# Fused Linformer attention and maxout MLP: one activation table set, even tokens first in batch 0, E and F by the plain queue, attention over both PSUM pools

## The chip, the cores and the metric

The kernel runs on one core of one Trainium2 chip. The metric is the device time of one execution in microseconds (us). A run's span is the part of it that the profiler sees, from the first instruction to the last. PE is TensorE (matmuls; PEld its weight loads), ACT is ScalarE, DVE is VectorE, POOL is GpSimd, SP is SyncE. A DMA issued by POOL goes through the software queue, which can convert fp32 to fp16 on the way; one issued by SP goes through the hardware queue and copies bytes as they are (the "plain queue").

## What is computed

Linformer attention over 8 batches and 8 heads, and behind it a maxout MLP on the 8192 tokens.

```python
# q, k, v: (8, 8, 1024, 64) fp32; E, F: (64, 1024); w1, w2: (512, 1024); w_out: (1024, 512)
k_proj = np.einsum('ks,bhsd->bhkd', E, k)
v_proj = np.einsum('ks,bhsd->bhkd', F, v)
scores = (1.0 / np.sqrt(64)) * np.matmul(q, k_proj.transpose(0, 1, 3, 2))
scores = scores - np.max(scores, axis=-1, keepdims=True)
attn = np.exp(scores)
attn = attn / (np.sum(attn, axis=-1, keepdims=True) + 1e-09)
attn_out = np.matmul(attn, v_proj)
x = attn_out.transpose(0, 2, 1, 3).reshape(8192, 512)
out = np.maximum(x @ w1, x @ w2) @ w_out        # (8192, 512) fp32
```

## The kernel before

All matmuls are fp16 with fp32 sums in PSUM. The order on every engine is the order in which the program is written (`manual_schedule`); semaphores follow from the tiles that instructions share.

**Attention of one batch** has these steps. `step_kv` (line 127): 16 matmuls give `k_proj` in partitions 0 to 63 and `v_proj` in 64 to 127 of one PSUM tile; ACT casts the first to `kp`, DVE the second, twice, to both halves of `vp`. `step_kpt` (line 145) transposes `kp` on PE; ACT and DVE copy it to `kpt`. Then for each of four pairs of heads p: `step_qt` (line 162) transposes the pair's q by eight PE transposes and DVE copies it to `qt`; `step_sc` (line 179) makes the scores with four matmuls and ACT takes their exponential to `ex`; `step_da` (line 195) makes the denominators (matmuls with a matrix of ones, into `dn_ps`) and the unnormalised result (into `at_ps`). The reciprocal is exp(-ln(x)): ACT computes `ld` (line 212, Ln) and `rec` (line 213, Exp). The multiply on DVE into `xt` (line 216) is returned as `finish` and is put into the program later. Token s is at partition s//8 and chunk s%8; the last axis but one of `xt` is the token's parity: even chunks at 0, odd chunks at 1.

**The MLP of one batch** is 24 blocks (`moe_blocks`, line 223), twelve for the even tokens (j=0), then twelve for the odd ones (j=1). An up block is eight matmuls, four for `w2` and four for `w1`, into two PSUM banks; ACT copies the first bank to `h2` (line 241), DVE takes the maximum with the second (line 242) into `gt`. After eight up blocks come four down blocks of eight matmuls (line 250), an ACT copy to `o_sb` (line 257) and an output DMA by SP. So blocks 0 to 7 and 12 to 19 are up, 8 to 11 and 20 to 23 down.

**PSUM** has eight banks in two rings. Tag "mm": four tiles of one bank, taken by MLP blocks alone. Tag "att": two tiles of two banks, taken in turn by every attention step, the transposes included. A new tile waits until the readers of the tile that had its place are done.

**The order.** Ahead of the loop the whole attention of batch 0 runs by itself, in two groups of four heads, pair after pair, each finished before the next begins (the head of the program). Then batch b's MLP blocks run, and between them stand the attention steps of batch b+1, by the table `plan` (block number to steps); a `finish` comes after the next block. The kernel's last batch has no attention beside it. POOL issues E and F first (lines 66, 67), then k, v, q of batch 0 in halves of four heads (line 76), the weights (line 92, in eight pieces; line 96), then builds the identity matrix for the transposes, and then loads the next batches as their buffers come free.

Of the kernel before, what the change touches and what calls it, by code (L numbers as in the profile page):

```python
# [8 lines left out]
FP32 = mybir.dt.float32  # L9
FP16 = mybir.dt.float16  # L10
ACTF = mybir.ActivationFunctionType
ALU = mybir.AluOpType
# [3 lines left out]
def kernel(  # L16
# [24 lines left out]

    scale = 1.0 / float(D) ** 0.5
# [3 lines left out]
    proj = ctx.enter_context(tc.tile_pool(name="proj", bufs=2))  # L46
    soft = ctx.enter_context(tc.tile_pool(name="soft", bufs=2))
    xpool = ctx.enter_context(tc.tile_pool(name="xpool", bufs=2))
    gpool = ctx.enter_context(tc.tile_pool(name="gpool", bufs=2))
# [40 lines left out]
    for f0 in range(0, DF, 256):  # L90
        for w_sb, w in ((w1_sb, moe_w1), (w2_sb, moe_w2)):
# [6 lines left out]
    ident16 = const.tile([128, 128], FP16)  # L98
    make_identity(nc, ident16)
    ones16 = const.tile([128, D], FP16)  # L100
    nc.vector.memset(ones16, 1.0)


    eft = const.tile([128, 2, NC, KP], FP16)
    ef_v = ef_sb.rearrange("kp i (p c) -> kp i c p", c=NC)
    eft_ps = att_banks(FP16)
    for i in range(2):
        for c in range(NC):
            nc.tensor.transpose(  # L109
                out=eft_ps[:, i, c * KP : (c + 1) * KP],  # L110
                in_=ef_v[:, i, c, :],
                identity=ident16[:KP, :KP],
            )
        nc.vector.tensor_copy(
            out=eft[:, i, :, :].rearrange("p c k -> p (c k)"), in_=eft_ps[:, i, 0 : NC * KP]
        )

# [8 lines left out]

    def step_kv(t, h0=0, h1=None):
        h1 = H if h1 is None else h1
        n = (h1 - h0) * D
        kv_ps = att_banks()  # L130
        for c in range(NC):
            nc.tensor.matmul(  # L132
                out=kv_ps[0:KP, 0, 0:n], lhsT=eft[:, 0, c, :], rhs=t["k"][:, h0:h1, c, :],
                start=(c == 0), stop=(c == NC - 1),
            )
            nc.tensor.matmul(  # L136
                out=kv_ps[KP:128, 0, 0:n], lhsT=eft[:, 1, c, :], rhs=t["v"][:, h0:h1, c, :],
                start=(c == 0), stop=(c == NC - 1),
            )
        fl = lambda ap: ap.rearrange("p h d -> p (h d)")  # L140
        nc.scalar.copy(out=fl(t["kp"][:, h0:h1, :]), in_=kv_ps[0:KP, 0, 0:n])  # L141
        nc.vector.tensor_copy(out=fl(t["vp"][KP:128, h0:h1, :]), in_=kv_ps[KP:128, 0, 0:n])
        nc.vector.tensor_copy(out=fl(t["vp"][0:KP, h0:h1, :]), in_=kv_ps[KP:128, 0, 0:n])

    def step_kpt(t, p0=0, p1=None):
        p1 = NP2 if p1 is None else p1
        kpt_ps = att_banks(FP16)
        for p in range(p0, p1):
            nc.tensor.transpose(
                out=kpt_ps[:, 0, p * KP : (p + 1) * KP],  # L150
                in_=t["kp"][:, 2 * p : 2 * p + 2, :],
                identity=ident16[:KP, :KP],
            )
        src = kpt_ps[:, 0, 0 : NP2 * KP].rearrange("q (p k) -> q p k", k=KP)
        dst = t["kpt"].rearrange("q (p e) k -> q p e k", e=2)
        for e in range(2):
            for r in range(2):
                eng = nc.scalar.copy if e == 0 else nc.vector.tensor_copy
                eng(
                    out=dst[r * D : (r + 1) * D, p0:p1, e, :],  # L160
                    in_=src[e * D : (e + 1) * D, p0:p1, :],
                )

    def step_qt(t, p):
        qt_ps = att_banks(FP16)
        for e in range(2):
            for i in range(NI):
                nc.tensor.transpose(  # L168
                    out=qt_ps[:, 0, (e * NI + i) * 128 : (e * NI + i + 1) * 128],
                    in_=t["q"][:, 2 * p + e, 2 * i : 2 * i + 2, :],  # L170
                    identity=ident16,
                )
        qt = soft.tile([128, 2, HALF], FP16, tag="qt", name="qt_sb")
        t["qt"][p] = qt
        nc.vector.tensor_copy(out=qt.rearrange("q e n -> q (e n)"), in_=qt_ps[:, 0, :])  # L175

    def step_sc(t, p):
        sc_ps = att_banks()  # L180
        qt = t["qt"].pop(p)
        for o in range(2):
            for e in range(2):
# [6 lines left out]
                )  # L190
        ex = soft.tile([128, 2, HALF], FP16, tag="ex", name="ex_sb")
        t["ex"][p] = ex
        nc.scalar.activation(out=ex, in_=sc_ps, func=ACTF.Exp, scale=scale)  # L193

    def step_da(t, p):
# [19 lines left out]
        def finish():  # L215
            nc.vector.tensor_tensor(  # L216
                out=t["xt"][:, p, :, :], in0=at_ps, in1=rec, op=ALU.mult
            )

# [66 lines left out]

    for b in range(B):
# [7 lines left out]
        for n, block in enumerate(moe_blocks(b, tiles[b])):  # L295
            block()
            if pending is not None:
                pending()
                pending = None
            if nxt is None:  # L300
                continue
            for s in plan.get(n, ()):
                if isinstance(s, tuple):
                    r = s[0](nxt, s[1])
                else:
                    r = s(nxt)
                if r is not None:
                    pending = r
# [31 lines left out]
```

## Time and profile before

| | |
|---|---|
| time, median of 3 runs | 506.37 us (505.75 to 507.42) |
| time of the profiled execution | 505.09 us |
| its span | 503.1 us |
| instructions | 5945 |
| HBM read, written | 57.15 MB, 16.78 MB |
| software queue (POOL's loads) | 30432 packets, 28.58 MB, 36.8% of 16 engines' span |
| hardware queue (SP's stores) | 9216 packets, 16.78 MB, 8.7% |
| PE matmuls of the up blocks (L234) | 1024, 382 ns each |
| PE matmuls of the down blocks (L250) | 512, 379 ns each |
| ACT table loads (L212 and L213) | 32 and 32, 1283 ns each |

Matmuls are pipelined: one begins while the one before still drains, so a row's duration is longer than the step from one to the next. The "idle before" of a row is the time that its engine stood with nothing running ahead of it, and the name behind the arrow is what ended that. A timeline row gives the start, the time, the engine, line and operation, the tiles (written<-read), shapes and count.

### The profile page before, as it was taken

The page shows a single profiled execution, that of the slowest core. Times are in us where ns is not written, and L with a number is a line of the kernel's source. Part 1 is how long each engine was busy: PE and PEld are TensorE (multiplying, and loading weights), DVE is VectorE, ACT ScalarE, POOL GpSimd, SP SyncE. Part 2 cuts the span into 40 slices and gives each one's busy share as a digit, 9 for nine tenths or more (in the row PEclk, how much of TensorE's full clock was granted, in tenths as well). Part 3 has the DMA queues.
Part 4 walks back from the last instruction along what each step waited for, and adds up shares of the span by engine and source line. Part 5 has one row for each costly group of instructions (what it writes and reads, how often), then busy time and mean ns, then how long its engine had stood idle before and what let it go on. Part 6 is the DMA issues. An engine that isn't in the chain of part 4 may idle for free.

```text
span 503.1 us, 5945 instructions
## 1 busy us (share of the span) xinstructions
PE 416.8 (83%) x2368; PEld 181.7 (36%) x2368; DVE 162.5 (32%) x231; ACT 296.7 (59%) x380; POOL 31.5 (6%) x44
## 2 busy tenths in 40 slices
PE   0053379888997999888988999889988999799997
PEld 0032124333443344333433344333433344334443
DVE  0023225242514334233524243242524252342231
ACT  1036644788367753887366854876467845866332
POOL 6321000000100010000100010000000000000000
PEclk9999999999999999999999999999999999999999
DMA  8999949233761629152751549152020011102112
GB/s 127 201 201 207 207 79 165 87 45 77 130 126 43 97 77 169 76 78 90 111 120 24 103 96 177 44 83 85 0 85 1 22 63 43 42 1 83 43 42 83
DMA packets 39675, 45.73 MB, mean 91 GB/s; under 512 B 1632, under 2 KB 31328, under 8 KB 39648
## 3 DMA queue, kind: packets, MB, share of 16 engines
q0 software_dynamic: 30432, 28.58, 36.8%
q1 hardware_dynamic: 9216, 16.78, 8.7%
q8 instruction: 18, 0.29, 0.2%
q14 instruction: 9, 0.07, 0.0%
HBM read 57.15 MB, written 16.78 MB: 147 GB/s over the span
## 4 chain that ended last, share of the span: by engine, by line
PE 48%; ACT 28%; issue 11%; DVE 8%; DMA 3%; POOL 1%; ACTq 0%; POOLq 0%
PE mm_ps L234 32%; PE mm_ps L250 8%; ACT L212 8%; ACT ld_sb L212 7%; DVE xt_sb L216 6%; ACT rec_sb L213 5%; DMA w_sb<-in_moe_w_dram 3%; PE att_ps L168 3%; ACT h_sb L241 3%; PE att_ps L132 3%; ACT ex_sb L193 2%; ACT o_sb L257 2%; ACT L213 1%; PE att_ps L185 1%; DVE gt_sb L242 1%
## 5 line engine op out<-in xcount | busy, mean ns | idle before, releaser
L234 PE MATMUL mm_ps<-xt_sb,w_sb 128*128 128x512 f16 x1024 | 238.1, 382 | 4.6 <-DVE xt_sb L216 4.0
L234 PEld LDWEIGHTS <-w_sb 128*128 128x128 f16 x1024 | 95.7, 98 | 126.4 <-issue 24.2
L242 DVE TENSOR_TENSOR gt_sb<-mm_ps,h_sb 128x512 f16<-128x512 f32 x128 | 88.4, 691 | 159.8 <-PE mm_ps L234 100.0
L241 ACT COPY h_sb<-mm_ps 128x512 f32<-128x512 f32 x128 | 74.8, 584 | 91.0 <-PE mm_ps L234 91.0
L250 PE MATMUL mm_ps<-wo_sb,gt_sb 128*128 128x512 f16 x512 | 118.0, 379 | 8.5 <-DVE gt_sb L242 5.5
L216 DVE TENSOR_TENSOR xt_sb<-att_ps,rec_sb 128x1024 f16<-128x1024 f32 x32 | 39.1, 1221 | 121.9 <-ACT rec_sb L213 121.9
L250 PEld LDWEIGHTS <-gt_sb 128*128 128x128 f16 x512 | 48.0, 98 | 73.5 <-issue 12.3
L257 ACT COPY o_sb<-mm_ps 128x512 f32<-128x512 f32 x64 | 35.9, 584 | 46.7 <-PE mm_ps L250 46.7
L193 ACT ACTIVATE ex_sb<-att_ps 128x1024 f16<-128x1024 f32 x32 | 32.9, 1027 | 14.9 <-PE att_ps L185 14.9
L213 ACT ACT_TABLE_LOAD x32 | 41.1, 1283 | 0.6
L212 ACT ACT_TABLE_LOAD x32 | 41.1, 1283 | 0.6
L168 PE MATMUL att_ps<-ident,q_sb 128*128 128x128 f16 x256 | 21.1, 229 | 22.9 <-DVE xt_sb L216 9.7
L213 ACT ACTIVATE rec_sb<-ld_sb 128x1024 f32<-128x1024 f32 x32 | 33.8, 1057 | 0.4
L212 ACT ACTIVATE ld_sb<-att_ps 128x1024 f32<-128x1024 f32 x32 | 32.8, 1024 | 0.4
L168 PEld LDWEIGHTS <-q_sb 128*128 128x128 f16 x256 | 18.2, 102 | 33.5 <-issue 28.4
L141 ACT CAST kp_sb<-att_ps 64x512 f16<-64x512 f32 (+1 forms) x9 | 4.8, 530 | 42.9 <-PE att_ps L136 42.9
L185 PE MATMUL att_ps<-qt_sb,kpt_sb 64*64 64x512 f16 x128 | 14.0, 426 | 12.5 <-DVE qt_sb L175 8.2
L175 DVE COPY qt_sb<-att_ps 128x1024 f16<-128x1024 f16 x32 | 21.9, 684 | 6.1 <-PE att_ps L168 6.1
L109 PE MATMUL att_ps<-ident,ef_sb 64*128 64x64 f16 x16 | 1.3, 241 | 26.1 <-POOL ident masks.py:199 25.6
L132 PE MATMUL att_ps<-k_sb,eft 128*64 128x512 f16 (+1 forms) x72 | 17.4, 390 | 1.3 <-ACT ld_sb L212 1.3
L76 POOL DMA_DIRECT2D q_sb<-in_q_dram x9 | 7.7, 855 | 163.3 <-PE att_ps L168 162.8
L204 PE MATMUL att_ps<-ex_sb,ones 64*64 64x512 f16 x128 | 14.0, 427 | 4.5 <-ACT ex_sb L193 4.5
(29 smaller groups left out, 114.4 us busy)
## 6 DMA issues: line engine op xcount, KB each, us to landing
out_dram<-o_sb SPq DMA_DIRECT2D x64, 256.0 KB, 2.0
k_sb<-in_k_dram POOLq DMA_DIRECT2D x7, 1024.0 KB, 9.3
v_sb<-in_v_dram POOLq DMA_DIRECT2D x7, 1024.0 KB, 14.0
q_sb<-in_q_dram POOLq DMA_DIRECT2D x7, 1024.0 KB, 9.4
w_sb<-in_moe_w_dram POOLq DMA_DIRECT2D x8, 256.0 KB, 14.6
k_sb<-in_k_dram POOLq DMA_DIRECT2D x2, 512.0 KB, 10.0
v_sb<-in_v_dram POOLq DMA_DIRECT2D x2, 512.0 KB, 11.8
q_sb<-in_q_dram POOLq DMA_DIRECT2D x2, 512.0 KB, 13.6
```

What stands on the lines that cost most here:

```text
L132: nc.tensor.matmul(out=kv_ps[0:KP, 0, 0:n], lhsT=eft[:, 0, c, :], rhs=t["k"][:, h0:h1, c, :], start=(c == 0), stop=(c == NC - 1),)
L168: nc.tensor.transpose(out=qt_ps[:, 0, (e * NI + i) * 128 : (e * NI + i + 1) * 128], in_=t["q"][:, 2 * p + e, 2 * i : 2 * i + 2, :], identi ...
L175: nc.vector.tensor_copy(out=qt.rearrange("q e n -> q (e n)"), in_=qt_ps[:, 0, :])
L193: nc.scalar.activation(out=ex, in_=sc_ps, func=ACTF.Exp, scale=scale)
L212: nc.scalar.activation(out=ld, in_=dn_ps, func=ACTF.Ln)
L213: nc.scalar.activation(out=rec, in_=ld, func=ACTF.Exp, scale=-1.0)
L216: nc.vector.tensor_tensor(out=t["xt"][:, p, :, :], in0=at_ps, in1=rec, op=ALU.mult)
L234: nc.tensor.matmul(out=h_ps, lhsT=w_sb[:, r, fb * 128 : (fb + 1) * 128], rhs=xt[:, r, j, :], start=(r == 0), stop=(r == NDC - 1),)
L241: nc.scalar.copy(out=h2, in_=banks[0])
L242: nc.vector.tensor_tensor(out=gt[:, fb, :], in0=banks[1], in1=h2, op=ALU.max)
L250: nc.tensor.matmul(out=op_ps, lhsT=gt[:, fb, i * 128 : (i + 1) * 128], rhs=wo_sb[:, fb, :], start=(fb == 0), stop=(fb == NFB - 1),)
L257: nc.scalar.copy(out=o_sb, in_=op_ps)
```

## The change

**Tables.** ACT loads one table set (number 6, with Ln and Exp) by hand as its first instruction. **E and F** come as fp32 by SP's queue, are transposed as fp32, and cast to fp16 as they leave PSUM, E's by DVE and F's by ACT. **The identity** is built after the first two loads that POOL issues; DVE makes its fp16 copy. **Batch 0's loads** are k and v in halves, then q in four pieces of two heads; for each slice of weights `w2` comes ahead of `w1`. **PSUM.** `step_kv`, `step_kpt`, `step_qt` and the transposes of E and F take a bank of the "mm" ring; scores and denominators keep the "att" ring. **Batch 0's attention** runs for all eight heads at once; the steps for pair p+1 stand ahead of the second half of pair p; and ahead of the MLP only the even tokens are finished, by `step_da_half` (denominators and result in one tile, half as wide). The odd tokens of pair n follow behind MLP block n. `ex` has four buffers for that. **The plan**: `step_kv` moves from block 1 to 4, `step_kpt` from 3 to 6, and most later steps by one to four blocks.

```diff
-    def mm_bank():
-        return ps.tile([128, 512], FP32, tag="mm", bufs=4, name="mm_ps")
-
-    def att_banks(dtype=FP32):
+    def mm_bank(dtype=FP32):
         return ps.tile(
-            [128, 2, 512 if dtype == FP32 else 1024], dtype, tag="att", bufs=2, name="att_ps"
+            [128, 512 if dtype == FP32 else 1024], dtype, tag="mm", bufs=4, name="mm_ps"
         )
 
+    def att_banks():
+        return ps.tile([128, 2, 512], FP32, tag="att", bufs=2, name="att_ps")
...
+    nc.scalar.add_instruction(
+        mybir.InstLoadActFuncSet(
+            name=nc.get_next_instruction_name(),
+            act_func_set_id=LN_EXP_SET,
...
-    ef_sb = const.tile([KP, 2, S], FP16)
-    nc.gpsimd.dma_start(out=ef_sb[:, 0, :], in_=E)
-    nc.gpsimd.dma_start(out=ef_sb[:, 1, :], in_=F)
+    ef_sb = const.tile([KP, 2, S], FP32)
+    nc.sync.dma_start(out=ef_sb[:, 0, :], in_=E)
+    nc.sync.dma_start(out=ef_sb[:, 1, :], in_=F)
...
-        load(tiles[0], "q", q, 0, h0, h0 + H // 2)
+        if h0 == 0:
+            ident = const.tile([128, 128], FP32)
+            make_identity(nc, ident)
+    for h0 in range(0, H, 2):
+        load(tiles[0], "q", q, 0, h0, h0 + 2)
...
+    def step_da_half(t, p, o):
+        ex = t["ex"][p]
+        da_ps = att_banks()
+        for i in range(2):
+            for e in range(2):
+                r = o ^ e
+                rows = slice(r * KP, (r + 1) * KP)
+                nc.tensor.matmul(
+                    out=da_ps[e * D : (e + 1) * D, i, :],
+                    lhsT=t["vp"][rows, 2 * p + e, :] if i else ones16[rows, :],
+                    rhs=ex[rows, e, :],
+                    start=True, stop=True,
+                )
+        ld = soft.tile([128, HALF], FP32, tag="ldh", name="ldh_sb")
+        rec = soft.tile([128, HALF], FP32, tag="rech", name="rech_sb")
+        nc.scalar.activation(out=ld, in_=da_ps[:, 0, :], func=ACTF.Ln)
+        nc.scalar.activation(out=rec, in_=ld, func=ACTF.Exp, scale=-1.0)
+
+        def finish():
+            nc.vector.tensor_tensor(
+                out=t["xt"][:, p, o, :], in0=da_ps[:, 1, :], in1=rec, op=ALU.mult
+            )
...
-    hh = H // 2
-    fins = []
-    for g in range(2):
-        step_kv(t, g * hh, (g + 1) * hh)
-        step_kpt(t, g * hh // 2, (g + 1) * hh // 2)
-        for p in range(g * hh // 2, (g + 1) * hh // 2):
-            step_qt(t, p)
-            step_sc(t, p)
-            step_da(t, p)()
-
+    step_kv(t)
+    step_kpt(t)
+    step_qt(t, 0)
+    step_sc(t, 0)
+    for p in range(NP2):
+        if p + 1 < NP2:
+            step_qt(t, p + 1)
+            step_sc(t, p + 1)
+        step_da_half(t, p, 0)()
+
+    first = {n: (step_da_half, n, 1) for n in range(NP2)}
     plan = {
-        1: [step_kv], 3: [step_kpt],
-        4: [(step_qt, 0)], 6: [(step_sc, 0)], 7: [(step_qt, 1)], 9: [(step_da, 0)],
-        10: [(step_sc, 1)], 11: [(step_qt, 2)], 13: [(step_da, 1)],
-        14: [(step_sc, 2)], 15: [(step_qt, 3)], 17: [(step_da, 2)],
+        4: [(step_kv,)], 6: [(step_kpt,)], 7: [(step_qt, 0)], 8: [(step_sc, 0)],
+        9: [(step_qt, 1)], 11: [(step_da, 0)], 12: [(step_sc, 1)], 13: [(step_qt, 2)],
+        14: [(step_da, 1)], 15: [(step_sc, 2)], 16: [(step_qt, 3)], 17: [(step_da, 2)],
         18: [(step_sc, 3)], 20: [(step_da, 3)],
     }
```

**What moves, on POOL.** These are POOL's first rows of the program before, from the second transfer on (the first is E's, L66); `ident_108` is the fp16 identity, whose two instructions are those of masks.py.

```order
L67 DMA ef_sb<-in_F_dram 64x1024
L76 DMA k_sb<-in_k_dram 128x4x512
L76 DMA v_sb<-in_v_dram 128x4x512
L76 DMA q_sb<-in_q_dram 128x4x512
L76 DMA k_sb<-in_k_dram 128x4x512
L76 DMA v_sb<-in_v_dram 128x4x512
L76 DMA q_sb<-in_q_dram 128x4x512
L92 DMA w_sb<-in_moe_w_dram 128x4x256 x8
L96 DMA wo_sb<-in_moe_w_out_dram 128x8x512
masks.py:197 MEMSET ident_108 128x128
masks.py:199 ISA
masks.py:199 AFFINE_SELECT ident_108<-ident_108 128x128
```

The same place in the changed program:

```order
L89 DMA k_sb<-in_k_dram 128x4x512
L89 DMA v_sb<-in_v_dram 128x4x512
masks.py:197 MEMSET ident 128x128
masks.py:199 ISA
masks.py:199 AFFINE_SELECT ident<-ident 128x128
L89 DMA k_sb<-in_k_dram 128x4x512
L89 DMA v_sb<-in_v_dram 128x4x512
L89 DMA q_sb<-in_q_dram 128x2x512 x4
L109 DMA w_sb<-in_moe_w_dram 128x4x256 x8
L113 DMA wo_sb<-in_moe_w_out_dram 128x8x512
```

The identity moved from behind seventeen transfers to behind two, the second half of v from seventh place in POOL's queue to fourth, and E and F left the queue.

**On ACT, in the head.** Before, one pair of heads after another (two of the four pairs are shown):

```order
L193 ACTIVATE ex_sb<-att_ps 128x1024
L212 ACT_TABLE_LOAD
L212 ACTIVATE ld_sb<-att_ps 128x1024
L213 ACT_TABLE_LOAD
L213 ACTIVATE rec_sb<-ld_sb 128x1024
L193 ACTIVATE ex_sb<-att_ps 128x1024
L212 ACT_TABLE_LOAD
```

And now, from the first exponentials on (`ldh` and `rech` are the half-width tiles of `step_da_half`):

```order
L205 ACTIVATE ex_sb<-att_ps 128x1024 x2
L250 ACTIVATE ldh_sb<-att_ps 128x512
L251 ACTIVATE rech_sb<-ldh_sb 128x512
L205 ACTIVATE ex_sb<-att_ps 128x1024
L250 ACTIVATE ldh_sb<-att_ps 128x512
L251 ACTIVATE rech_sb<-ldh_sb 128x512
L205 ACTIVATE ex_sb<-att_ps 128x1024
```

The table loads are gone, the logarithm and the reciprocal are half as wide, and the exponential of pair p+1 stands ahead of those of pair p.

**On ACT, in the loop**, from the last down blocks of the even tokens into the up blocks of the odd ones. Before:

```order
L257 COPY o_sb<-mm_ps 128x512 x2
L212 ACT_TABLE_LOAD
L212 ACTIVATE ld_sb<-att_ps 128x1024
L213 ACT_TABLE_LOAD
L213 ACTIVATE rec_sb<-ld_sb 128x1024
L257 COPY o_sb<-mm_ps 128x512
L193 ACTIVATE ex_sb<-att_ps 128x1024
L257 COPY o_sb<-mm_ps 128x512
L241 COPY h_sb<-mm_ps 128x512 x2
```

And now:

```order
L295 COPY o_sb<-mm_ps 128x512 x3
L224 ACTIVATE ld_sb<-att_ps 128x1024
L225 ACTIVATE rec_sb<-ld_sb 128x1024
L279 COPY h_sb<-mm_ps 128x512
L205 ACTIVATE ex_sb<-att_ps 128x1024
L279 COPY h_sb<-mm_ps 128x512 x2
L224 ACTIVATE ld_sb<-att_ps 128x1024
```

The first `step_da` moved from behind block 9 to behind block 11, its two table loads are gone, and one MLP block still stands between it and the next scores.

More of the change, by code (lines that the diff above doesn't have):

```diff
@@ L10 @@
 FP16 = mybir.dt.float16
+LN_EXP_SET = 6
 ACTF = mybir.ActivationFunctionType
@@ L90 @@
     for f0 in range(0, DF, 256):
-        for w_sb, w in ((w1_sb, moe_w1), (w2_sb, moe_w2)):
+        for w_sb, w in ((w2_sb, moe_w2), (w1_sb, moe_w1)):
             nc.gpsimd.dma_start(
@@ L96 @@
     nc.gpsimd.dma_start(out=wo_sb, in_=moe_w_out.rearrange("(r p) f -> p r f", p=128))
[L98 to L99 removed]
     ones16 = const.tile([128, D], FP16)
     nc.vector.memset(ones16, 1.0)
+    ident16 = const.tile([128, 128], FP16)
+    nc.vector.tensor_copy(out=ident16, in_=ident)
     eft = const.tile([128, 2, NC, KP], FP16)
     ef_v = ef_sb.rearrange("kp i (p c) -> kp i c p", c=NC)
[L106 removed]
     for i in range(2):
+        eft_ps = mm_bank()
         for c in range(NC):
             nc.tensor.transpose(
[L110 removed]
+                out=eft_ps[:, c * KP : (c + 1) * KP],
                 in_=ef_v[:, i, c, :],
[L112 removed]
+                identity=ident[:KP, :KP],
             )
[L114 to L116 removed]
+        eng = nc.scalar.copy if i else nc.vector.tensor_copy
+        eng(out=eft[:, i, :, :].rearrange("p c k -> p (c k)"), in_=eft_ps)
     def new_attn(t):
@@ L125, in new_attn, with step_kv, step_kpt @@
         t["ex"] = {}
[L127 to L130, printed above, removed]
+    def step_kv(t):
+        kv_ps = mm_bank()
         for c in range(NC):
[L132 to L139, printed above, removed]
-        fl = lambda ap: ap.rearrange("p h d -> p (h d)")
[L141 to L148, printed above, removed]
+            for i, n in enumerate(("k", "v")):
+                nc.tensor.matmul(
+                    out=kv_ps[i * KP : (i + 1) * KP, :],
+                    lhsT=eft[:, i, c, :],
+                    rhs=t[n][:, :, c, :],
+                    start=(c == 0), stop=(c == NC - 1),
+                )
+        fl = lambda ap: ap.rearrange("p h d -> p (h d)")
+        nc.scalar.copy(out=fl(t["kp"]), in_=kv_ps[0:KP, :])
+        nc.vector.tensor_copy(out=fl(t["vp"][KP:128]), in_=kv_ps[KP:128, :])
+        nc.vector.tensor_copy(out=fl(t["vp"][0:KP]), in_=kv_ps[KP:128, :])
+    def step_kpt(t):
+        kpt_ps = mm_bank(FP16)
+        for p in range(NP2):
             nc.tensor.transpose(
-                out=kpt_ps[:, 0, p * KP : (p + 1) * KP],
+                out=kpt_ps[:, p * KP : (p + 1) * KP],
                 in_=t["kp"][:, 2 * p : 2 * p + 2, :],
@@ L190, in step_sc @@
                 )
-        ex = soft.tile([128, 2, HALF], FP16, tag="ex", name="ex_sb")
+        ex = stage.tile([128, 2, HALF], FP16, tag="ex", name="ex_sb")
         t["ex"][p] = ex
@@ L299 @@
                 pending = None
+            if b == 0 and n in first:
+                s = first[n]
+                pending = s[0](tiles[0], *s[1:])
             if nxt is None:
```

26 lines of the change are left out of this document (16 added, 10 removed).

## The prediction

> **What bounds the kernel now.** First the busy times with the span cut at the places where the MLP of a batch gets its last input (the start of the matmuls that wait for the fourth pair's `xt`): the head in two rows, the first batch, one of six equal ones, and the last with the tail.
>
> ```profile
> 0.00:25.60 25.60, 0.01 (x1) 0.14 (x2) 0.11 (x1) 1.28 (x1) 13.25 (x24) 1.00 1.07 165
> 25.60:68.00 42.40, 18.33 (x136) 9.85 (x136) 10.94 (x18) 24.34 (x26) 5.16 (x6) 1.00 1.26 203
> 67.97:125.26 57.29, 52.56 (x292) 22.27 (x292) 20.05 (x28) 36.58 (x47) 2.63 (x3) 1.00 0.43 79
> 180.81:236.37 55.56, 50.83 (x293) 21.87 (x293) 20.05 (x28) 36.73 (x48) 2.62 (x3) 1.00 0.48 95
> 458.57:503.10 44.53, 40.95 (x189) 18.38 (x188) 11.07 (x16) 14.22 (x25) 0.00 (x0) 0.98 0.17 65
> ```
>
> Columns are the stretch and its length, busy time of PE, PEld, DVE, ACT and POOL, the granted clock, DMA share and GB/s. There are two programs in one: a head of 68 us in which PE works 18 us, and a loop in which PE works 50.8 of 55.6 us and everything else has room (ACT 36.7, DVE 20.1). In the loop only PE's idle time can go; in the head nearly all can. So next, what PE waits for (us in total, times, longest):
>
> ```profile
> PE att_ps L109 <- POOL ident masks.py:199: 25.6, 1, 25.6
> PE att_ps L168 <- DVE xt_sb L216: 9.7, 7, 1.4
> PE att_ps L168 <- ACT ex_sb L193: 9.5, 7, 1.4
> PE mm_ps L250 <- DVE gt_sb L242: 5.5, 7, 0.8
> PE att_ps L185 <- ACT ld_sb L212: 4.3, 7, 0.6
> PE mm_ps L234 <- DVE xt_sb L216: 4.0, 4, 3.5
> PE mm_ps L250 <- ACT h_sb L241: 3.0, 7, 0.4
> ```
>
> 25.6 us go to the identity, which POOL builds behind all of the first loads. Five waits come seven times each, once per batch with attention beside it: 9.7 + 9.5 + 5.5 + 4.3 + 3.0 = 32.0 us. The timeline shows their cause, with a stretch without a wait for comparison:
>
> ```profile
> 195.07 0.41 PE L185 MATMUL att_ps<-qt_sb,kpt_sb 64*64 64x512 f16 x4
> 195.41 1.90 PE L234 MATMUL mm_ps<-xt_sb,w_sb 128*128 128x512 f16 x8
> 197.15 0.61 PE L168 MATMUL att_ps<-ident,q_sb 128*128 128x128 f16 x8
> ...
> 201.15 0.41 PE L204 MATMUL att_ps<-ex_sb,ones 64*64 64x512 f16 x4
> 201.70 1.90 PE L250 MATMUL mm_ps<-wo_sb,gt_sb 128*128 128x512 f16 x8
> 201.86 1.28 ACT L212 ACT_TABLE_LOAD   x1
> 203.15 1.02 ACT L212 ACTIVATE ld_sb<-att_ps 128x1024 f32<-128x1024 f32 x1
> 204.22 0.41 PE L185 MATMUL att_ps<-qt_sb,kpt_sb 64*64 64x512 f16 x4 [0.62 <-ACT ld_sb L212]
> 205.49 1.06 ACT L213 ACTIVATE rec_sb<-ld_sb 128x1024 f32<-128x1024 f32 x1
> 206.57 1.22 DVE L216 TENSOR_TENSOR xt_sb<-att_ps,rec_sb 128x1024 f16<-128x1024 f32 x1 [7.86 <-ACT rec_sb L213]
> 207.85 0.61 PE L168 MATMUL att_ps<-ident,q_sb 128*128 128x128 f16 x8 [1.38 <-DVE xt_sb L216]
> ```
>
> Unhindered, eight matmuls take 1.74 us from start to start (195.41 to 197.15) although the row says 1.90; the 0.16 between is drain that overlaps. So each wait costs 0.16 more than its row says. With table loads between, ACT needs 4.7 us from 201.86 to hand `rec` to DVE, and PE stands at every "att" tile that has to come free.
>
> **The change: the loop.** The five waits are 32.0/7 = 4.57 us a batch, plus 5 x 0.16 = 5.37. The matmuls that open a batch wait too: (4.0 - 3.5)/3 = 0.17, plus 0.16. Together 5.7 us a batch; 55.56 - 5.7 leaves 49.86. PE's own instructions per batch stay the same, only their places change.
>
> Are the waits gone, and what is late next? I walk the queues with the durations above. (1) Scores behind `ld`: the denominators take 0.41 from 201.15; an ACT copy of 0.58 goes ahead, ready 0.2 later by the drain, so `ld` runs 0.8 to 1.8 after the first of these matmuls. PE wants that tile one block later, at 0.55 + 1.74 = 2.29. Early by 0.5. (2) The q transposes leave the "att" ring. They now wait for the bank that is four allocations back: for the third pair, behind block 13, that is the `h2` bank of block 12, free when ACT has done `ld`, `rec` (1.06) and the copy (0.58), at 3.5; wanted two blocks and the scores later, at 4.37. Early by 0.9. (3) Down block 20, the next late one: its eighth matmul needs `gt` of block 19. From the third pair's denominators: `rec` until 2.5, copy of block 18 until 3.1, maximum (0.69) until 3.85, the multiply (1.22) until 5.1, maximum of block 19 until 5.8. PE comes to it after two blocks and the scores, 4.37, and seven matmuls, 1.52: 5.89. Early by under 0.1. It costs nothing by this walk, but a delay on DVE there is paid in full, seven times. MLP blocks share their ring with six more tiles a batch; the tightest reuse is the first bank of a block that takes the `w1` bank of two blocks before, 1.74 us after it is filled; the maximum is normally done 0.16 + 0.69 later, so DVE may be 0.9 late. The multiplies take 1.22 but stand behind that maximum in DVE's queue, so I cost the sharing at nothing. Seven batches: **-39.9 us**.
>
> **The change: the head.** Rows for its links (issue and landing of the two transfers that fix them, the durations at full width, and one pair of before):
>
> ```profile
> 4.65 0.79 POOL L76 DMA_DIRECT2D k_sb<-in_k_dram  x1
> k_sb<-in_k_dram POOLq DMA_DIRECT2D x1, 512.0 KB, 12.7
> L109 PE MATMUL att_ps<-ident,ef_sb 64*128 64x64 f16 x16 | 1.3, 241 | 26.1 <-POOL ident masks.py:199 25.6 <-DVE eft L114 0.5
> 26.72 0.88 POOL L76 DMA_DIRECT2D v_sb<-in_v_dram  x1 [0.33 <-DMA w_sb<-in_moe_w_dram]
> v_sb<-in_v_dram POOLq DMA_DIRECT2D x1, 1024.0 KB, 21.6
> 67.97 4.70 PE L234 MATMUL mm_ps<-xt_sb,w_sb 128*128 128x512 f16 x13 [3.50 <-DVE xt_sb L216]
> L141 ACT CAST kp_sb<-att_ps 64x512 f16<-64x512 f32 x7 | 4.1, 579 | 15.0 <-PE att_ps L136 15.0
> L142 DVE CAST vp_sb<-att_ps 64x512 f16<-64x512 f32 x7 | 4.9, 694 | 12.0 <-ACT kp_sb L141 12.0
> L159 DVE COPY kpt_sb<-att_ps 64x256 f16<-64x256 f16 x14 | 4.1, 293 | 1.5 <-ACT kpt_sb L159 1.4
> L175 DVE COPY qt_sb<-att_ps 128x1024 f16<-128x1024 f16 x32 | 21.9, 684 | 6.1 <-PE att_ps L168 6.1
> L241 ACT COPY h_sb<-mm_ps 128x512 f32<-128x512 f32 x128 | 74.8, 584 | 91.0 <-PE mm_ps L234 91.0
> L242 DVE TENSOR_TENSOR gt_sb<-mm_ps,h_sb 128x512 f16<-128x512 f32 x128 | 88.4, 691 | 159.8 <-PE mm_ps L234 100.0
> 31.20 1.01 PE L168 MATMUL att_ps<-ident,q_sb 128*128 128x128 f16 x8 [0.61 <-DVE vp_sb L143]
> 41.41 0.64 PE L185 MATMUL att_ps<-qt_sb,kpt_sb 64*64 64x512 f16 x4 [3.21 <-DVE qt_sb L175]
> 42.10 1.02 ACT L193 ACTIVATE ex_sb<-att_ps 128x1024 f16<-128x1024 f32 x1 [2.60 <-PE att_ps L185]
> 47.86 1.23 DVE L216 TENSOR_TENSOR xt_sb<-att_ps,rec_sb 128x1024 f16<-128x1024 f32 x1 [6.50 <-ACT rec_sb L213]
> ```
>
> *Loads.* The identity is ready within 4 us; what ends last is then the second half of v. It stands fourth among k, v and q as k's second half did, which landed at 4.65 + 12.7 = 17.35. POOL reaches its first load sooner by two issues, at most 2 x 0.79 us; E and F as fp32 put twice their 0.26 MB into SBUF, some 1.3 us more at the 203 GB/s of the second window. I set the one against the other and take 17.4; the ends are 15.8 (the extra bytes are hidden) and 19.9 (none of the issue time comes back and E and F go ahead at full length). The Trainium skill, "Trainium Kernel Development and Optimization", section Key Constraints, says that DMAs issued from different engines run on the same 16 DMA engines and interleave, and that another queue only saves issue time. By it the bytes of E and F still count, which is the value taken; were SP's queue a second road, 15.8 would stand. Transposes of fp32 have no row; the 16 fp16 ones of L109 are 1.3 us of PE, and even five times that lies in PE's idle time between the identity and 17.4. That wait is their cover.
>
> *Chain.* In the head PE runs at half its pace: 13 matmuls take 4.70 us at 67.97, where the loop's 1.74 for eight makes 2.8, and four score matmuls take 0.64 instead of 0.41. So `step_kv`, eight pairs at twice 0.22, ends with its drain 3.8 after the landing, at 21.2. Then `kp` 0.58, two `vp` casts, 2 x 0.69, two `kpt` copies, 2 x 0.29, `qt` 0.68, scores 0.64: with 0.05 per hand-over the first exponential starts 4.1 later. The second follows 2.5 behind it (1.01 of transposes beside 1.02 of Exp, copy, scores). From there a pair takes Exp 1.02, `ld` and `rec` at half width, 2 x 0.58 (no row shows them; they lie between zero and the 1.02 of full width, and the nearest row is the copy of that width, 584 ns), multiply 0.69 (the nearest row, L242), `qt` 0.68, scores 0.64 and hand-overs: 4.35; before, the way from Exp to the end of the multiply alone took 42.10 to 49.09, 7.0. Two such, then Exp, four half-width ACT passes and a multiply, 4.1. Sum 4.1 + 2.5 + 8.7 + 4.1 = 19.4, so the MLP has its last even input at 40.6 instead of 67.97: **-27.4 us**. All eight half-width passes are on this chain: at 1.02 they add 3.5, at nothing they take 4.6 off. With the ends of the landing it lies between 34 and 47.
>
> *Beside the MLP.* The odd halves add four groups of four matmuls, each like the scores, 0.34 (195.07 to 195.41): **+1.4 us**. The next batch's v lands at 26.72 + 21.6 = 48.3; batch 0 asks for it five blocks in, at about 52. Weights land before that, so no transfer becomes late, with some 4 us in hand.
>
> **The sum** is made against the profiled execution: 503.1 - 39.9 - 27.4 + 1.4 = 437.2 us of span; around the span lie 505.09 - 503.1 = 2.0 us, so 439.2; the median of the runs is 1.3 above the profiled one: **440 us**.
>
> **The rivals.** *PE warms in the head.* The half pace shows in the durations of the head (the granted-clock column says 1.00 all the same), and the gaps ahead of its rows are 3.21 and 3.50 us. The new head has no gap over about 2 us. If PE ran at the loop's pace there, the scores would gain 0.23 in four pairs, and the first batch its extra 57.29 - 55.56 = 1.7: 2.7 us off, 437. For it: the shorter gaps. Against: PE stays barely half busy. The Trainium skill, "TensorE: Matmul & The Clock Gate", Part 1, puts the rule so: PE runs at half rate until some 3.4 us of sustained work, and falls back after as long a gap. By that the shorter gaps help only once it is warm.
>
> *A new wait in the loop.* ACT and DVE come late to the "mm" banks or to down block 20, because transposes and MLP now draw on one ring. For it: margins of 0.1 to 0.9. Against: with ACT at 36.7 - 8 x 1.28 = 26.5 of 50 us, delays don't pile up. If between a fifth and half of the 5.7 comes back, 7 x 1.1 to 7 x 2.9 = 8 to 20 us: 448 to 460.
>
> *The waits stay.* The loads go but PE's order, not ACT, made the waits: only the head gains, 480. Against it: the `ld` wait is half the length of one table load. The order of ACT shows a single load in the changed program, so that part does what it says.
>
> *Slower: the clock.* A loop without gaps could make the chip throttle PE. The gain of 66 us is lost when a loop of some 394 us (53.0 for the first batch, 6 x 49.86, 42 for the last) takes 17% longer; at the half pace of the head it would add over 300. Against it: the last batch ran 42 us with PE at work nearly throughout, at a granted 0.98. The same page of the Trainium skill says that a limit to 13/16 comes only with a third busy core on a die; no run here shows it.
>
> **Chances.** Forecast 0.62 (434 to 447, by the ends of the head); warm PE 0.12; new wait 0.20; waits stay 0.04; slower 0.02. The range takes the first two and the nearer half of the third: 434 to 455. A measurement tells 0.3% from no change; faster by more than that is 0.98, within it 0, slower 0.02.
>
> **What would show it.** In the changed profile: one ACT_TABLE_LOAD; the first `step_kv` matmul near 17.4; the MLP's 13-matmul row near 40.6; ex-to-ex steps of 4.35 in the head; a batch period of 49.9; no wait of PE that comes seven times, or else first the one of the down blocks on `gt`. I am wrong if the period stays above 51, if v lands past 20, or if a row of `ldh` is much longer than 0.6.

## The result and the profile after

| | before | changed |
|---|---|---|
| time, median | 506.06 us (504.67 to 507.42, 4 runs) | 439.42 us (439.28 to 439.81, 4 runs) |
| profiled execution, its span | 505.09, 503.1 us | 439.34, 437.6 us |
| ratio, 95% interval | | 0.8685 (0.866 to 0.8709) |

The change takes 66.6 us off. The same two views as before, of the changed kernel: stretches of the span (the first MLP, then one period of the loop, from the matmuls right behind one batch's `step_kv` to the same place of the next), and what PE waits for (the five longest of eight rows).

```profile
38.80:92.37 53.57, 53.57 (x305) 21.91 (x305) 22.25 (x32) 30.30 (x46) 2.64 (x3) 1.00 1.09 196
102.95:152.89 49.94, 49.94 (x295) 21.77 (x293) 19.86 (x28) 26.43 (x39) 2.63 (x3) 1.00 0.53 106
```

```profile
PE mm_ps L147 <- DMA k_sb<-in_k_dram: 6.6, 1, 6.6
PE att_ps L197 <- DVE qt_sb L187: 5.7, 4, 1.8
PE mm_ps L126 <- DMA ef_sb<-in_E_dram: 4.6, 1, 4.6
PE mm_ps L147 <- DMA v_sb<-in_v_dram: 1.9, 1, 1.9
PE mm_ps L272 <- DVE xt_sb L254: 0.7, 1, 0.7
```

The second column of the stretches (the length) and the first busy time (PE) are now the same number: by this profile PE never stands still in the loop. All five waits that came seven times are gone; every wait that is left lies in the head. There, the timeline of PE and ACT (a choice of its rows) shows the chain that the prediction walked:

```profile
16.10 0.60 PE L147 MATMUL mm_ps<-v_sb,eft 128*64 128x512 f16 x1 [1.89 <-DMA v_sb<-in_v_dram]
19.73 0.58 ACT L154 CAST kp_sb<-mm_ps 64x512 f16<-64x512 f32 x1 [12.10 <-PE mm_ps L147]
23.72 1.02 ACT L205 ACTIVATE ex_sb<-att_ps 128x1024 f16<-128x1024 f32 x1 [2.17 <-PE att_ps L197]
26.11 1.02 ACT L205 ACTIVATE ex_sb<-att_ps 128x1024 f16<-128x1024 f32 x1 [1.37 <-PE att_ps L197]
30.35 1.02 ACT L205 ACTIVATE ex_sb<-att_ps 128x1024 f16<-128x1024 f32 x1 [2.07 <-PE att_ps L197]
34.59 1.02 ACT L205 ACTIVATE ex_sb<-att_ps 128x1024 f16<-128x1024 f32 x1 [2.07 <-PE att_ps L197]
36.77 0.60 ACT L250 ACTIVATE ldh_sb<-att_ps 128x512 f32<-128x512 f32 x1
38.80 2.29 PE L272 MATMUL mm_ps<-xt_sb,w_sb 128*128 128x512 f16 x5 [0.67 <-DVE xt_sb L254]
41.03 0.63 PE L242 MATMUL att_ps<-ex_sb,ones 64*64 64x512 f16 x2
42.02 2.06 PE L272 MATMUL mm_ps<-xt_sb,w_sb 128*128 128x512 f16 x8
44.01 0.40 PE L242 MATMUL att_ps<-ex_sb,ones 64*64 64x512 f16 x2
44.25 0.38 PE L242 MATMUL att_ps<-ex_sb,vp_sb 64*64 64x512 f16 x2
44.56 1.90 PE L272 MATMUL mm_ps<-xt_sb,w_sb 128*128 128x512 f16 x8
```

The MLP has its last input at 38.80 instead of 67.97.

### The profile page after: what moved, and what is told of

The parts are those of the page before. It is cut to its first block, busy times and chain, and to the rows that moved or that the text cites. A ratio compares the mean times of both kernels' runs of the same rounds, so it can differ in the third digit from the quotient of the medians.

```text
span 437.6 us, 5860 instructions
## 1 busy us (share of the span) xinstructions
PE 413.1 (94%) x2352; PEld 180.3 (41%) x2352; DVE 160.7 (37%) x231; ACT 215.4 (49%) x322; POOL 31.8 (7%) x44
## 4 chain that ended last, share of the span: by engine, by line
PE 92%; DMA 3%; ACT 2%; DVE 1%; issue 1%; POOL 1%; POOLq 0%
PE mm_ps L272 52%; PE mm_ps L288 26%; PE mm_ps L147 4%; PE att_ps L216 4%; PE mm_ps L180 3%; PE att_ps L197 3%; DMA v_sb<-in_v_dram 3%; ACT ex_sb L205 1%; DVE qt_sb L187 1%; PE att_ps L242 1%; ACT rech_sb L251 1%; ACT ldh_sb L250 1%; PE mm_ps L161 0%; POOL k_sb L89 0%; DVE xt_sb L254 0%
## 5 line engine op out<-in xcount | busy, mean ns | idle before, releaser
L228 DVE TENSOR_TENSOR xt_sb<-att_ps,rec_sb 128x1024 f16<-128x1024 f32 x28 | 34.1, 1217 | 24.7 <-ACT rec_sb L225 24.7
L187 DVE COPY qt_sb<-mm_ps 128x1024 f16<-128x1024 f16 x32 | 21.9, 683 | 25.8 <-PE mm_ps L180 25.7
L225 ACT ACTIVATE rec_sb<-ld_sb 128x1024 f32<-128x1024 f32 x28 | 29.6, 1057 | 0.9
L147 PE MATMUL mm_ps<-k_sb,eft 128*64 128x512 f16 x64 | 17.2, 413 | 6.6 <-DMA k_sb<-in_k_dram 6.6
L180 PE MATMUL mm_ps<-ident,q_sb 128*128 128x128 f16 x256 | 21.2, 230 | 0.0
L147 PE MATMUL mm_ps<-v_sb,eft 128*64 128x512 f16 x64 | 17.0, 413 | 1.9 <-DMA v_sb<-in_v_dram 1.9
L154 ACT CAST kp_sb<-mm_ps 64x512 f16<-64x512 f32 x8 | 4.6, 579 | 26.9 <-PE mm_ps L147 26.9
L89 POOL DMA_DIRECT2D k_sb<-in_k_dram x9 | 7.8, 864 | 116.2 <-PE mm_ps L147 114.2
L155 DVE CAST vp_sb<-mm_ps 64x512 f16<-64x512 f32 x8 | 5.6, 694 | 25.4 <-ACT kp_sb L154 25.4
L147 PEld LDWEIGHTS <-eft 128*64 128x64 f16 x128 | 7.3, 116 | 17.7 <-issue 13.4
## 6 DMA issues: line engine op xcount, KB each, us to landing
v_sb<-in_v_dram POOLq DMA_DIRECT2D x2, 512.0 KB, 10.3
```

The costliest lines, as they stand in the source:

```text
L147: nc.tensor.matmul(out=kv_ps[i * KP : (i + 1) * KP, :], lhsT=eft[:, i, c, :], rhs=t[n][:, :, c, :], start=(c == 0), stop=(c == NC - 1),)
L180: nc.tensor.transpose(out=qt_ps[:, (e * NI + i) * 128 : (e * NI + i + 1) * 128], in_=t["q"][:, 2 * p + e, 2 * i : 2 * i + 2, :], identity= ...
L225: nc.scalar.activation(out=rec, in_=ld, func=ACTF.Exp, scale=-1.0)
L228: nc.vector.tensor_tensor(out=t["xt"][:, p, :, :], in0=at_ps, in1=rec, op=ALU.mult)
```

## The experiments

Two questions were open although the time had come out as forecast: which of its parts earned it, and what bounds the head now. Each run is of its own kernel; ratios are to the kernel before on the same chip. The kernel before is called B, the changed one C.

| kernel | time, us | ratio to B, 95% interval |
|---|---|---|
| B with one table set | 458.85 | 0.9072 (0.9056 to 0.9088) |
| C without it | 485.77 | 0.9612 (0.959 to 0.9635) |
| C, attention on the "att" ring | 438.54 | 0.8687 (0.8654 to 0.8721) |
| C with the old plan | 442.74 | 0.8759 (0.8737 to 0.8781) |
| C, no split by parity | 441.78 | 0.8736 (0.8723 to 0.8749) |
| C, E and F by POOL | 440.22 | 0.8711 (0.8695 to 0.8726) |
| B, identity first | 490.81 | 0.9704 (0.9686 to 0.9721) |
| C, PE kept busy until 16 us | 437.91 | 0.866 (0.8636 to 0.8683) |
| C in two groups of heads | 433.48 | 0.8575 (0.8556 to 0.8595) |
| the same, PE kept busy in the whole head | 434.74 | 0.8588 (0.8566 to 0.861) |
| the same, batch 1's attention later | 429.62 | 0.8485 (0.8468 to 0.8503) |
| C again, beside the last one | 439.06 | 0.8675 (0.8652 to 0.8698) |

### One table set alone, and all but the table set

```diff
 # B
+    nc.scalar.add_instruction(mybir.InstLoadActFuncSet(act_func_set_id=LN_EXP_SET, ...))
 # and C
-    nc.scalar.add_instruction(mybir.InstLoadActFuncSet(act_func_set_id=LN_EXP_SET, ...))
```

> The kernel before with one edit: ACT loads the joint table set at its start, so the 64 later loads (1.283 us each) are gone; rings, plan, loads and head are those of before. Theory T (the five loop waits of PE come from ACT being late by the loads): walked with the durations of the trace before, the scores, the q transposes and down block 20 all come to a free tile, so 7 x 5.6 = 39 us go, and in the head 8 loads on the chain, 10.3 us: about 457. Rival R (the waits come from attention having only the two att tiles): the loop keeps its period of 55.5 and only the head's 10.3 go: about 496.

> The changed kernel without the table set loaded by hand: the loads of Ln and Exp come back (two for each Ln and Exp pair, 72 and one at the start), everything else stays. T: the eight loads of the head's even halves are on its chain (+10.3), and in the loop ld and rec are 2.6 us later, so the scores behind ld wait about 0.8, the q transposes for the bank of a late h copy about 1, and down block 20 for gt about 1.7: 4 to 6 us a batch, 28 to 42; about 480 to 490. R: the rings carry the gain, the loop hardly changes: about 450.

Measured: 458.85 and 485.77. First the loop period of each (B with one set, then C without it), then what PE of C without the set waits for:

```profile
120.75:170.69 49.94, 49.94 (x293) 21.76 (x292) 20.04 (x28) 26.54 (x39) 2.62 (x3) 1.00 0.52 106
```

```profile
126.38:180.76 54.38, 51.14 (x293) 21.92 (x293) 19.67 (x28) 36.66 (x47) 2.62 (x3) 1.00 0.50 97
```

```profile
PE mm_ps L169 <- ACT h_sb L268: 7.2, 14, 0.6
PE mm_ps L277 <- DVE gt_sb L269: 5.5, 7, 0.8
PE att_ps L186 <- ACT ld_sb L213: 4.3, 7, 0.6
PE mm_ps L277 <- ACT h_sb L268: 3.0, 7, 0.4
```

With its rings, plan and order untouched, B needs only the table set to reach exactly C's period of 49.94. C without the set stands at 54.38, and its q transposes wait twice a batch for an "mm" bank that a late `h2` copy frees (7.2 in 14), in place of the "att" tiles of before. So taking out the table loads is enough to remove all of the loop's waits. As long as the loads are there, the rings and the plan together save 1.2 us a batch (55.56 to 54.38) and decide where the lateness shows; no run took those two apart with the loads in place. In B's head the set took off less than the 10.3 us expected: the MLP had its last input at 60.52, 7.4 sooner. Of the two loads of a pair, the one ahead of Ln had partly stood beside the matmuls that make the denominators (in B the load began at 43.14 and they began at 43.17).

### The rings and the plan

```diff
 # C, attention on the "att" ring
-        kv_ps = mm_bank()
+        kv_ps = att_banks()[:, 0, :]
-        kpt_ps = mm_bank(FP16)
+        kpt_ps = att_banks(FP16)[:, 0, :]
-        qt_ps = mm_bank(FP16)
+        qt_ps = att_banks(FP16)[:, 0, :]
 # C with the old plan
-        4: [(step_kv,)], 6: [(step_kpt,)], 7: [(step_qt, 0)], 8: [(step_sc, 0)],
+        1: [(step_kv,)], 3: [(step_kpt,)], 4: [(step_qt, 0)], 6: [(step_sc, 0)],
...
```

> The changed kernel with kv, kpt and q transposes back in the two att tiles (as before the change); tables, plan, head order and loads stay. T: without table loads the tiles come free in time in the loop, at most 1 us a batch is lost, and the head's chain loses some us because the next pair's transposes wait for a tile: 441 to 450. R: the loop's waits come back, 4 us a batch or more: 465 or more.

> The changed kernel with the plan of before (kv behind block 1, first denominators behind block 9). T: in the loop no wait, period 49.9; in the first batch kv stands at about 43 us and waits for v of the next batch, which lands at about 47 to 48: 4 to 5 us once: about 444. Rival P (the new places in the plan keep PE free of waits): 1 to 5 us a batch: 447 to 475.

Measured: 438.54, not to be told from C and below the 441 to 450 that was expected, and 442.74. The loop's period is 49.94 in both; neither part does anything there. The head of the first lost less than expected: from the last half of v to the MLP's last input it took 23.35 us (15.56 to 38.91), C 22.70. The old plan costs 3.7 us once, where `step_kv` of batch 1 is too early for its load (PE's timeline, C with the old plan):

```profile
43.48 0.40 PE L147 MATMUL mm_ps<-k_sb,eft 128*64 128x512 f16 x1
47.62 0.38 PE L147 MATMUL mm_ps<-v_sb,eft 128*64 128x512 f16 x1 [3.74 <-DMA v_sb<-in_v_dram]
```

So the new plan is worth 3.3 us by the times and 3.7 by this wait, through its move of `step_kv` in the first batch.

### The parts of the head

```diff
 # C, no split by parity
-        step_da_half(t, p, 0)()
+        step_da(t, p)()
-    first = {n: (step_da_half, n, 1) for n in range(NP2)}
+    first = {}
 # C, E and F by POOL (transposed as fp16)
-    ef_sb = const.tile([KP, 2, S], FP32)
-    nc.sync.dma_start(out=ef_sb[:, 0, :], in_=E)
+    ef_sb = const.tile([KP, 2, S], FP16)
+    nc.gpsimd.dma_start(out=ef_sb[:, 0, :], in_=E)
...
 # B, identity first: these two lines ahead of the first load
+    ident16 = const.tile([128, 128], FP16)
+    make_identity(nc, ident16)
```

> The changed kernel without the split by parity: the head finishes even and odd tokens of a pair together with the full-width step, and nothing of batch 0's attention is left beside its MLP. Theory H (the split pays because the half-width passes shorten the head's chain): eight ACT passes at 1.03 and 1.06 instead of 0.60 and 0.63 (+3.4) and three multiplies on the chain at 1.22 instead of 0.69 (+1.6) against four half steps of 0.55 to 1.0 less beside the MLP (-2.65): 441 to 443. Rival: the half steps cost PE as much as full ones (0.55 each in the changed profile), so the split gains nothing: 438 to 440.

> The changed kernel with E and F as fp16 through POOL's queue again, ahead of k and v; the identity stays early. If the two issues of POOL time count in full, the last v lands 1.2 us later than 16.1 and the time rises by 1.2: 440.6. If only bytes count (0.26 MB fewer), it lands up to 1.3 earlier: 438.1. My working of the prediction set the two against each other: about 439.4, v within 0.5 of 16.1.

> The kernel before with one edit: the identity is built ahead of all loads. If the 25.5 us wait was the identity's alone, PE now waits for the first half of v (landed at 12.3, about 0.5 later now), so the first pairs run some 15 us sooner; the second group's k and v land by 20.4, in time. Head ends at 67.97 - 15 = 53: about 491. Rival: loads end the head anyway (v of the second half, weights): the gain is below 8: 498 or more.

Measured: 441.78, 440.22 and 490.81. The split is worth 2.4 us by the times. The traces agree: without it the way from the last half of v to the MLP's last input takes 27.61 us (17.36 to 44.97) instead of 22.70 (16.10 to 38.80), 4.9 more, and the 2.6 us of the odd halves are saved. Moving two lines so that POOL builds the identity first takes 14.9 us off B (505.68 on that chip, less 490.81). In B so changed, PE waits for v until 12.98 (last row below) instead of for the identity until 25.6.

For E and F the time does not decide: the runs spread from 438.53 to 440.95, and C's own from 437.3 to 440.9 beside the last experiment. Nor does the landing of v. PE's timeline of the kernel with E and F by POOL, of C without the split (the same chip, with C's loads), then of B with the identity first:

```profile
17.56 0.60 PE L147 MATMUL mm_ps<-v_sb,eft 128*64 128x512 f16 x1 [1.90 <-DMA v_sb<-in_v_dram]
```

```profile
17.36 0.61 PE L147 MATMUL mm_ps<-v_sb,eft 128*64 128x512 f16 x1 [1.90 <-DMA v_sb<-in_v_dram]
```

```profile
4.43 0.70 PE L110 MATMUL att_ps<-ident,ef_sb 64*128 64x64 f16 x8 [4.43 <-DMA ef_sb<-in_E_dram]
12.98 0.37 PE L137 MATMUL att_ps<-v_sb,eft 128*64 128x256 f16 x1 [2.29 <-DMA v_sb<-in_v_dram]
```

With E and F on POOL the last half of v comes at 17.56, where C's first profile has 16.10. But six profiles with C's loads, issued at the same time to 0.01 us, have it anywhere from 15.56 to 17.36. What the trace does show is the issue: POOL gives out that half of v at 5.23 us instead of 4.17, so the two issues for E and F cost POOL 1.06 us, where 1.2 had been expected. How much of that reaches the landing, and whether the bytes give some of it back, these runs do not show.

### PE's pace, and a shorter head

```diff
 # C, PE kept busy until 16 us; nobody reads warm_ps
+    for _ in range(32):
+        nc.tensor.matmul(out=warm_ps, lhsT=ident16, rhs=warm, start=True, stop=True)
```

> The changed kernel with 32 matmuls that nobody reads, put on PE between the transposes of E and F (about 7 us) and the wait for v (16.1). If the head's half pace is PE's clock after idling, kv runs at full pace (-1.6) and, if PE stays warm, the scores gain 0.23 in four pairs (-0.9), the first MLP matmuls 1.4 to 1.7, the half steps 0.4: 434.8 to 437.8. If the half pace has another cause, or PE is cold again after kv: 437.8 to 439.4; if the 32 matmuls run cold throughout they end at 21 and cost 4: 443.

Measured: 437.91, which the intervals do not tell from C. PE's timeline of this kernel:

```profile
6.81 9.81 PE L139 MATMUL mm_ps<-warm,ident 128*128 128x512 f16 x32 [0.18 <-DVE warm L136]
17.16 0.38 PE L153 MATMUL mm_ps<-v_sb,eft 128*64 128x512 f16 x1
22.17 0.41 PE L203 MATMUL att_ps<-qt_sb,kpt_sb 64*64 64x512 f16 x4 [1.83 <-DVE qt_sb L193]
22.51 0.97 PE L186 MATMUL mm_ps<-ident,q_sb 128*128 128x128 f16 x8
24.26 0.64 PE L203 MATMUL att_ps<-qt_sb,kpt_sb 64*64 64x512 f16 x4 [0.78 <-DVE qt_sb L193]
```

The matmuls of `step_kv` take 0.38 here, in C 0.63 (16.92); the first scores run in 0.41, the second in 0.64. So the matmuls that nobody reads brought PE to full pace, and within a few microseconds of the chain it was lost again. The half pace is then a matter of how busy PE has lately been, as the rival "PE warms in the head" had it, but the head as it is cannot hold it. Next, the head in two groups, with and without matmuls that keep PE busy in all of its waits, and then with batch 1's attention later:

```diff
 # two groups: k, v, q of heads 0 to 3 are loaded first, then those of heads 4 to 7
+    for g in range(2):
+        p0 = g * NP2 // 2
+        step_kv(t, g * hh, (g + 1) * hh)
+        step_kpt(t, p0, p0 + NP2 // 2)
+        for p in (p0, p0 + 1):
+            step_qt(t, p)
+            fill(3 if p % 2 else 6)      # only where PE is kept busy
+            step_sc(t, p)
+        for p in (p0, p0 + 1):
+            step_da_half(t, p, 0)()
 # batch 0's plan, in the first two (the rest as in C)
+        6: [(step_kv,)], 7: [(step_kpt,)], 8: [(step_qt, 0)], 9: [(step_sc, 0)], 10: [(step_qt, 1)],
 # in the third
+        8: [(step_kv,)], 9: [(step_kpt,)], 10: [(step_qt, 0)],
+        11: [(step_sc, 0), (step_qt, 1)], 12: [(step_da, 0)], 13: [(step_sc, 1)],
...
```

> The changed kernel with batch 0's attention in two groups of four heads again (k, v and q of the first four heads land first; both pairs of a group in flight together), and batch 1's kv, kpt and first q steps one or two blocks later so that they meet their loads. If the last half of v bounds the start of the chain (16.1 in the changed profile), the first group starts at about 11.2 and its pairs run while the second group lands; the MLP begins at about 32.4 instead of 38.8: about 433. If the second group's k and v (now landing behind two pieces of q, about 18.7), or the longer chain of two kv steps, end the head instead: 437 to 440.

> As e9_groups, with matmuls that nobody reads in PE's waits of the head (12 ahead of the first kv, 3 or 6 behind each pair's transposes, 2 behind every other half step), so that PE is nowhere idle for long. If PE's pace in the head is set by how busy it has been lately, kv, scores and the first MLP matmuls run at full pace: 2 to 4.5 us below e9_groups. If it stays cold, the fillers run at half pace and delay the chain: 0 to 2 above it.

Measured: 433.48 and 434.74. The first came as expected. The second gained nothing (the intervals overlap): it lies among the 0 to 2 us above that were set down for a PE that stays cold, but PE was at full pace. Its PE timeline says where the gain went:

```profile
25.50 0.41 PE L211 MATMUL att_ps<-qt_sb,kpt_sb 64*64 64x512 f16 x4
30.05 1.24 PE L286 MATMUL mm_ps<-xt_sb,w_sb 128*128 128x512 f16 x5 [0.77 <-DVE xt_sb L268]
47.95 0.59 PE L160 MATMUL mm_ps<-v_sb,eft 128*64 128x512 f16 x1 [3.35 <-DMA v_sb<-in_v_dram]
51.46 2.85 PE L286 MATMUL mm_ps<-xt_sb,w_sb 128*128 128x512 f16 x8
```

The head did what was wanted: full pace throughout (0.41), and the MLP's last input at 30.05, where the groups alone had it at 33.27. But now PE reaches `step_kv` of batch 1 before that batch's v has landed, waits 3.35 us, and loses its pace on top: the 16 matmuls of `step_kv` take 3.5 us (47.95 to 51.46) and the next eight 2.85.

> As e10_groups_warm, with batch 1's attention two blocks later in batch 0's MLP (kv behind block 8), so that kv meets v of batch 1, which landed at 47.9 there. In e10 PE waited 3.35 us for it and ran the next matmuls at half pace (kv 3.5 instead of 1.85 us, eight matmuls 2.8 instead of 1.74). If that wait is what ate the gain of the earlier head (its MLP began at 30.1 against 33.3 in e9_groups), 5 to 6 us come off e10's 434.7: 429 to 430. If loads bound the first 50 us in another way (q, or the weights of the down blocks), 432 to 435.

> The changed kernel itself, on the same chip as e11_late_kv, for the distance between the two: 439.4 within 1.

Measured: 429.62, and 439.06 for C beside it. PE's timeline around the same place has no wait left:

```profile
30.66 1.24 PE L286 MATMUL mm_ps<-xt_sb,w_sb 128*128 128x512 f16 x5 [0.77 <-DVE xt_sb L268]
46.44 1.89 PE L302 MATMUL mm_ps<-wo_sb,gt_sb 128*128 128x512 f16 x8
50.11 1.90 PE L302 MATMUL mm_ps<-wo_sb,gt_sb 128*128 128x512 f16 x8
```

Between the two down blocks stand eight matmuls' 1.8 us and a `step_kv` of 1.85. The two kernels differ in batch 0's plan alone, so the load of v was what had eaten the gain. This kernel is 9.4 us faster than the changed one.

## Why the prediction was right, point by point

- **The loop.** Forecast 5.7 us a batch and a period of 49.86; measured 55.56 - 49.94 = 5.62. That the table loads made all five waits is shown by the run with the set alone. The walk of the queues held: at the tightest place, down block 20, the maximum of block 19 was forecast at 5.8 us after the third pair's denominators and the matmul that needs it at 5.89; in the trace of the changed kernel, by the rows below, the maximum ends 5.5 us after they begin (80.33 to 85.15 + 0.68 = 85.83), and block 20 (84.80) runs its eight matmuls in 1.89 without a wait.

```profile
80.33 0.41 PE L216 MATMUL att_ps<-ex_sb,ones 64*64 64x512 f16 x4
...
84.80 1.89 PE L288 MATMUL mm_ps<-wo_sb,gt_sb 128*128 128x512 f16 x8
85.15 0.68 DVE L280 TENSOR_TENSOR gt_sb<-mm_ps,h_sb 128x512 f16<-128x512 f32 x1
```

- **The loads in the head.** 17.4 was taken, 16.10 came in this profile. Six profiles with the same loads spread from 15.56 to 17.36, so the 1.3 us are in part chance, and 17.4 lies just past the latest of them. The step set POOL's saved issue time against the extra bytes of E and F. The rule of the Trainium skill, "Trainium Kernel Development and Optimization", section Key Constraints, that another queue saves issue time agrees with the traces (1.06 us on POOL); that the added bytes then cost time, which I took from it, no run here settles.
- **The chain.** Forecast and measured: landing to the end of `step_kv` 3.8 and 3.6, to the first exponential 4.1 and 4.0, to the second 2.5 and 2.4, then 4.35 and 4.24 a pair, and 4.1 and 4.2 to the MLP's last input. The half-width passes, which no row had shown, took 595 and 630 ns by the groups below; 584 had been taken.

```profile
L250 ACT ACTIVATE ldh_sb<-att_ps 128x512 f32<-128x512 f32 x8 | 4.8, 595 | 4.2 <-PE att_ps L242 4.2
L251 ACT ACTIVATE rech_sb<-ldh_sb 128x512 f32<-128x512 f32 x8 | 5.0, 630 | 0.3
```

- **The odd halves** were mis-sized: 4 x 0.34 = 1.4 forecast, 41.03 to 42.02 = 0.99 once and 44.01 to 44.56 = 0.55 three times measured, 2.6. I had priced them like the scores, four matmuls in 0.4. But the timeline shows the two matmuls with vp 0.24 behind the two with the ones (44.01 and 44.25), so a half step costs PE as much as a full one (0.55). By the code, the scores' four matmuls differ in the half of the partitions that they read or in the half that they write, while in the half step each matmul with vp reads and writes the same halves as one with the ones; that this makes the 0.24 is read from code and rows, no run took it apart. The first half step also ran at half pace (0.63 a row instead of 0.40), which is 0.4 of the 2.6.
- **The sum.** The span was forecast at 437.2 and is 437.6. The landing came 1.3 early and the chain was 0.5 shorter; the odd halves cost 1.2 more and the loop 7 x 0.08 = 0.6; the last 0.4 us belong to no term. That the errors cancelled is luck: the total is better than its terms.
- **The rivals.** The waits did not stay, and no new one came, though six more tiles drew on the "mm" ring. A slower clock did not come either: PE is busy 49.94 of 49.94 us and the matmuls step as before. PE did not warm in the head: all four scores of the profile take 0.64 (in C with E and F by POOL the first took 0.41, the other three 0.64).
- **What carried the change.** The table set gives 47 of the 67 us (506.06 to 458.85), the identity's place, which the title leaves out, 15 on its own; the split by parity 2.4 and the plan 3.3 in the changed kernel; spreading attention over both PSUM rings gives nothing that the runs can tell. Taking all eight heads at once, with the next pair's steps ahead, had no run of its own; two groups of heads, with both pairs of a group in flight, were 6 us faster (433.48).

## What to carry to other kernels

An engine that is busy two thirds of the time (ACT, 36.7 of 55.6 us) can still set the pace: look at which wait ends last in one period, and take out the piece of work that makes the engine late there, before rearranging the buffers in which the lateness shows. In a program's head, read the queue of the engine that issues the loads in order: a small operation behind many transfers can hold up everything. After each gain ask which load is next; a head that is shorter by 9 us met the next batch's load, and moving the next batch's attention by up to two blocks was worth 5. Before a landing is explained, see how far it moves between runs that have the same loads.

## What was not expected of the hardware

- PE's half pace comes back sooner than the waits suggest. In the run that kept PE busy until 16 us no wait behind the 32 matmuls is over 1.83 us, and still the scores fell from 0.41 to 0.64 (22.17 and 24.26). In the two groups with PE kept busy, the granted clock fell 2.0 us into the wait of 3.35 (44.60 to 47.95), as the stretches below say (the clock is the number behind POOL's); in C with the old plan a wait of 3.74 us left full pace behind it (0.38 at 47.62). So the length of a wait alone does not decide.

```profile
44.60:46.40 1.80, 0.01 (x1) 0.00 (x0) 0.47 (x1) 0.00 (x0) 0.00 (x0) 1.00 1.24 204
46.60:47.90 1.30, 0.00 (x0) 0.00 (x0) 0.00 (x0) 0.00 (x0) 0.00 (x0) 0.50 1.25 209
```

  The Trainium skill, "TensorE: Matmul & The Clock Gate", Part 1, gives an idle window of about 3.4 us as the condition, and here the clock fell after less; the same page, section "A second HAM failure mode: psum-queue depth-cycling", tells of a pace that swings because PE idles briefly and often, which is nearer to these rows. In the clock records of the traces, the shorter stretches between two changes of the clock last 3.41, 6.82, 10.24 or 13.65 us, whole multiples of 3.41. So it looks as if the clock is set at a fixed beat, and as if it counts where in the beat a wait falls; no run moved a wait to see. It also stays open whether the transposes between the waits count as work: between the last `step_kv` matmul and the scores PE did nothing but transposes and waiting. With the waits filled by matmuls, 0.41 held through the head.
- A granted clock of 1.00 does not always mean full pace. The clock rows of the pages, 40 slices of the span, first of C, then of the run that kept PE busy until 16 us:

```profile
PEclk9999999999999999999999999999999999999999
```

```profile
PEclk9958999999999999999999999999999999999999
```

  The second shows the loss (from 22.6 to 36.3 us by finer stretches). The first shows 9 throughout, although C's head runs at half pace: C's trace holds no clock record ahead of 42.4 us, and where there is none the row says full clock.
- When the pace comes back in the first MLP differs from run to run: the changed kernel's five matmuls behind the last input took 2.29 us in one profile (38.80) and 1.24 in the profile beside the last experiment (38.43). That kernel's time spread there from 437.3 to 440.9 us, over 0.8%; a change worth 1 us has to be read from the trace.
- Sixteen transposes of E and F in one row took 2.21 to 2.37 us in fp32 (C without the table set, C with the old plan) and 1.13 in fp16 (C with E and F by POOL): twice as long for elements of twice the size.
